# Per-buffer fills of the ones behind the probabilities, and a new issue order, in a fused attention and MLP kernel

## The chip, the core and the metric

The kernel runs on one core of a Trainium2 chip. The metric is the device time of one execution in microseconds (us). A core has a matrix engine (PE) that writes its products to eight accumulator banks, a vector engine (DVE), a scalar engine (ACT), a general engine (POOL) and a queue engine (SP) that only issues DMAs. Each engine takes its instructions strictly in the order in which the program lists them for it; engines wait for each other, and for DMAs, through semaphores.

## The reference

```python
scores = scale * np.matmul(q, k.transpose(0, 1, 3, 2))       # 4 batches, 8 heads, 768 x 64
# heads 0, 2, 6 ("retrieval"): causal mask
# other heads ("stream"): causal, and key < 4 or within 64 behind the query
a = softmax(where(mask, scores, -1e9))
x = matmul(a, v)                      # laid out as 3072 tokens x 512
h = x @ w_in                          # 512 -> 2048
g = np.maximum(h, 0.0) + alpha * np.minimum(h, 0.0)
out = g @ w_out                       # 2048 -> 512, float32
```

## The kernel before

The whole program is a list of small named steps, `ORDER`, written out by hand in the source. Each name is looked up in a table `I` and called, and the call emits the instructions of that step. As every engine is in order, `ORDER` fixes for each engine, and for the DMA queues of SP, ACT and POOL, what stands behind what. PSUM banks are handed out by age while the list is walked (`take`, `give`).

Heads are worked in pairs, four pairs for a batch: pair number n runs from 0 to 15, n modulo 4 chooses the heads (2,6), (1,5), (0,4) or (3,7), and n divided by 4 is the batch. The letters of a name tell the step:

- `Lq`, `Lk`, `Lv`: load q, k or v of a pair by DMA, nearly all from the SP queue, one or two DMAs for a head (L202 to L249). There are four buffers for each of the three. A stream head's v has a small extra DMA for its last 24 rows (L249), which waits for a fill of the buffer (`vz`).
- `Cq`, `Ck`, `Cv`: cast to bf16, on POOL for the first pairs, later mostly on DVE. A cast of v of a stream pair also copies the four sink rows (L312).
- `Tq`, `Tk`, then `tq`, `tk`: for n below 8, transpose on PE and copy out of the bank (DVE for the first pairs, ACT later). From n = 8 on, `Dq` and `Dk` do it by transposing DMAs on the SP queue (L328, L344).
- `S n.hh.m`, `s`, `m`: scores of a part on PE, exponential on ACT (L473, L521, L527), mask by a multiply on DVE. In batch 0 the scores use two pairs of banks in turn and the mask is added on PE. From n = 4 on, consecutive `S` steps are gathered into a burst; where both heads of the array's halves have enough columns, the burst interleaves them so that two 64-row products run side by side (L434), and otherwise it emits them one at a time (L427).
- `A`, `a`: probabilities times v on PE (L560), then reciprocal and multiply on DVE (L570, L571). The v tile has a column of ones, so the sum of each row comes with it.
- `X`, `x`: transpose the pair's result into `xT`, on PE with a copy on DVE (L585, L590), or by a transposing DMA on SP (L579) for n = 4 and 8 to 14.
- `P t.f`, `p`, `g`: for token block t (512 or 256 tokens, two blocks for a batch) and block f of 128 columns of w_in, four products on PE (L605), one for each head pair in the order (2,6), (1,5), (0,4), (3,7); then a relu on ACT (L610) and the combination on DVE (L617). For f below 6 of block 0 the four products are three steps: `.0` the first two pairs, `.1` the third, `.2` the fourth.
- `O t.s.u`, `o`: a quarter (four products) of the second matrix product (L625), and the copy and store of 128 tokens. `L0` to `L2` are the last 128 tokens in three column pieces (L644).
- `wi0` to `wi7`, `wo0` to `wo3`: the weights, by DMAs on the POOL queue that also convert to bf16 (L713, L717). `wi` number i holds columns 512*(i//2) and up, for one half of the 128 rows: `P t.4` to `P t.7` need `wi2` and `wi3`, `P t.0` to `P t.3` need `wi0` and `wi1`, and so on.
- `warm`, `busy`: products on a zero tile at the start. `kz`, `qz`, `vz`, `sz`, `vo`, `ro`, `so`, `nz`, `kfz`: fills of parts of buffers that no later step writes. `ms`, `mr`, `ns`, `nr`: masks.

`eR` (two buffers) and `eS` (three buffers) hold the probabilities of retrieval and stream heads. A product of a tile of 128 rows reads a few columns behind the last written one; those are filled with ones by `ro` and `so` at the start.

```python
    for name in ORDER:
        if not beside_burst(name):
            emit_burst()
        I[name]()
```

Of the kernel before, what the change touches and what calls it, by code (L numbers as in the profile page):

```python
# [11 lines left out]


ORDER = """
busy warm0 sz2 kz1 kz3 Lq0.0 zero Lq0.1 id kz0 Lk0 La kz2 Lk1 nms Cq0.0 nmr qz Tq0.0 Lq1 Ck0.0 qz0 warm1 Tk0.0 Lq2 Lk2
mr warm2 vz3 Ck0.1 Cq0.1 Ck1.1 tk0.0 m14.0.2 tq0.0 Lv0 Ck1.0 S0.0.1 Tk0.1 vz1 sz1 tk0.1 s0.0.1 Lk3 S0.0.0 Cq1 Tq0.1
Lv1 Cq2 vz0 Ck2.1 S0.0.2 Ck2.0 vz2 s0.0.0 tq0.1 Cv0 Ck3.0 Tk1 Lq3 Tq1 sz0 s0.0.2 Lq5 so tq1 S0.1.2 vo s0.1.2 S0.1.0
s0.1.0 Lv2 Tq2 S0.1.1 Ck3.1 tk1.0 tk1.1 S1.0.1 Tk2 s0.1.1 tk2.1 tk2.0 s1.0.1 S1.0.0 A0.0 Cv1 tq2 A0.1 a0.0 wi0 a0.1
s1.0.0 S2.1.1 S2.1.0 s2.1.1 Tk3 S2.0.0 Cq3 s2.1.0 m4.0.2 m10.0.2 X0 wi1 s2.0.0 Cv2 S2.0.1 S1.1.1 Cq5 x0 s2.0.1 Tq3
tk3.0 ro Lk4 s1.1.1 Ck4.1 S1.1.0 tk3.1 tq3 wi2 s1.1.0 A1.0 S2.0.2 A2.1 S3.1.1 a1.0 Lv3 Ck4.0 Cv3.0 a2.1 Lk5 A1.1  # L20
s2.0.2 idf s3.1.1 S3.1.0 A2.0 s3.1.0 S3.0.0 a1.1 X1 a2.0 S3.0.1 x1 s3.0.1 kfz1 s3.0.0 Tk4 Cv3.1 wi3 wi6 X2 m6.0.2 Tq5
x2 A3.1 P0.2.0 Lq6 tk4.0 a3.1 A3.0 P0.3.0 Ck5.0 Lq4 tk4.1 a3.0 wi7 P0.0.0 wi5 ms P0.1.0 Al kfz2 X3 Ck5.1 P0.1.1 Tk5
tq5 wi4 tk5.0 x3 P0.0.1 P0.2.1 P0.3.1 P0.1.2 P0.0.2 P0.3.2 Cq4 P1.2 al p0.1 g0.1 p0.3 Lk6 P0.2.2 P1.0 p0.2 g0.3 p1.0
g0.2 p0.0 g1.0 P1.6 P1.4 Lq8 p1.2 one Lq7 g1.2 nz1 wo1 nz0 Tq4 P0.6 wo0 P0.5.0 tk5.1 g0.0 P0.5.1 Lk7 P0.4.0 P0.4.1
p0.6 P0.4.2 g0.6 P0.5.2 p1.6 P0.14 g1.6 Cq6 Tq6 Ck6.0 p1.4 p0.14 g1.4 tq6 P0.13 p0.4 P0.10 g0.14 g0.4 p0.5 kfz0 P1.8
wo2 P0.9 Lv5 p0.13 tq4 g0.5 p1.8 g0.13 g1.8 p0.9 P0.11 Lv4 g0.9 p0.10 S4.0.4 S5.1.2 S4.1.3 Lv6 S4.0.0 p0.11 P1.10
s4.0.0 P0.8 P0.7 g0.10 g0.11 p1.10 S5.0.0 Lk9 g1.10 s5.1.2 p0.8 s4.0.4 g0.8 S4.1.1 S5.0.2 p0.7 S4.1.2 P0.12 s4.1.2 wo3
O0.1.0 s5.0.2 g0.7 s4.1.3 O0.1.1 Ck6.1 p0.12 S5.1.0 g0.12 m4.0.0 s4.1.1 S5.1.1 S4.0.3 m5.1.2 S5.0.1 Lq9 s5.0.0 S4.0.5
S4.1.4 Cv5 Cq7 s4.1.4 Lk8 m4.1.4 m5.0.0 Cq8 s5.0.1 P0.15 O0.3.0 s5.1.1 p0.15 s5.1.0 Tk6 Ck7.0 P1.14 g0.15 S4.1.5
s4.0.3 S4.0.1 s4.0.5 S4.1.0 S4.0.2 O0.3.1 O0.1.2 m5.1.1 m5.1.0 m4.0.4 s4.0.2 p1.14 m5.0.1 s4.1.0 Ck7.1 tk6.1 m4.1.3  # L30
m4.1.0 m5.0.2 O0.3.2 O0.0.0 tk6.0 Tk7 m4.1.1 A5.0 s4.0.1 A5.1 O0.0.1 g1.14 O0.0.2 Cv4 a5.0 Cv6 a5.1 Tq7 O0.3.3 tk7.0
O0.0.3 m4.0.3 O0.1.3 tk7.1 m4.0.5 m4.0.1 s4.1.5 o0.3 tq7 m4.1.5 o0.1 A4.1 S6.0.5 S7.0.0 o0.0 S6.1.2 S6.1.0 S7.0.2
S6.1.1 a4.1 A4.0 s6.1.1 S6.0.4 O0.2.0 s6.1.2 O0.2.1 s6.0.5 Lv7 m6.1.1 s7.0.0 s6.1.0 Cq9 Dq8 Ck8 m6.1.0 S6.0.0 s7.0.2
S7.1.0 s6.0.4 S7.1.2 S6.0.1 S7.1.1 S6.0.3 Dk8.0 m6.0.4 O0.2.2 s6.0.3 s7.1.0 m6.0.3 s7.1.2 X5 Dk8.1 P1.12 s6.0.1 m7.0.2
m6.1.2 Dq9 x5 m6.0.1 s7.1.1 m7.0.0 p1.12 Lv8 Ck9 a4.0 O1.1.0 m6.0.5 g1.12 Cv7 A6.1 ns s6.0.0 O0.2.3 S7.0.1 S6.0.2
m6.0.0 O1.1.1 S8.0.2 nr O1.1.2 s6.0.2 s7.0.1 Dk9.0 o0.2 A6.0 Lk10 S8.1.0 S8.0.1 m7.0.1 S8.0.3 s8.0.2 S8.1.1 S8.0.0
m7.1.0 a6.1 m7.1.1 S8.1.4 X4 s8.0.1 s8.1.4 a6.0 Dk9.1 Lq10 O1.1.3 s8.1.0 Lv9 A7.0 X6 m7.1.2 a7.0 kfz3 x6 s8.0.0 s8.1.1
A7.1 O1.0.0 O1.0.1 S9.0.0 S8.1.5 s8.0.3 S8.1.2 S9.0.2 o1.1 S8.0.4 a7.1 S8.1.3 X7 s8.1.3 Ck10 m8.1.0 s8.0.4 s8.1.5
O1.0.2 Lk11 s9.0.0 m8.0.3 O1.0.3 x7 P2.4 o1.0 m9.0.0 s8.1.2 S9.1.1 S9.0.1 m8.1.1 m8.1.5 p2.4 S9.1.2 S8.0.5 S9.1.0
m8.0.0 near0 m8.0.1 Lk13 s9.0.2 s8.0.5 s9.1.2 m8.0.4 P2.14 P2.2 s9.1.1 Cv8 s9.0.1 g2.4 m8.1.3 m8.1.4 A8.1 P3.10 P2.3  # L40
p2.2 P2.0 g2.2 Cq10 m8.0.5 a8.1 p2.14 g2.14 p2.0 m9.1.2 P2.1 g2.0 p2.3 P2.7 p2.7 p2.1 A8.0 P3.0 g2.3 P2.5 Ck11 g2.1
P2.9 p2.5 P2.6 g2.7 near2 g2.5 s9.1.0 p3.10 p3.0 p2.9 Cv9 g3.10 P2.8 Lq11 Dk11.1 g2.9 P3.8 m9.1.0 P2.10 p2.8 m9.1.1
Lk12 P3.4 g3.0 A9.1 near1 p2.6 g2.8 Lq13 P2.13 Cq11 P2.15 p2.13 Dk10.1 Dk10.0 Dq10 g2.6 p2.10 g2.13 p3.4 Lq12 P3.6
g2.10 P3.14 p2.15 a9.1 g2.15 P2.11 O2.0.0 P2.12 g3.4 O2.0.1 p2.11 p3.8 g2.11 Ck12 S10.0.1 S10.0.4 s10.0.1 g3.8 p3.14
O2.0.2 s10.0.4 Dk11.0 O2.1.0 Dq11 p2.12 a8.0 g3.14 S10.1.1 S10.0.0 p3.6 g2.12 m10.0.4 S10.1.0 S10.0.5 s10.1.0 s10.1.1
O2.1.1 Lv11 Cq12 O2.0.3 g3.6 S10.0.3 S11.0.0 m10.1.0 s10.0.5 s10.0.0 S11.1.2 S11.1.0 m9.0.2 S10.1.2 S10.0.2 s10.0.3
Cq13 O2.1.2 m10.0.0 s10.1.2 Lv10 Ck13 m9.0.1 m10.1.2 s11.1.2 m11.1.2 s11.1.0 Dk12.0 P3.2 s10.0.2 p3.2 A9.0 s11.0.0
# [24 lines left out]


@with_exitstack
def kernel(
    ctx: ExitStack,
    tc: tile.TileContext,
    q: bass.AP,
    k: bass.AP,
    v: bass.AP,  # L80
    is_retrieval: bass.AP,
# [652 lines left out]
    fill("qz", qT_all[:, :, S:S + 32].bitcast(fp32), 0.0)  # L734
    fill("qz0", qT_all[D:128, 0, 0:S].bitcast(fp32), 0.0)
    fill("vo", vb_all[:, :, :, :, D:D + 1], 1.0)
    fill("ro", eR_all[:, :, FAR.RTOT:E_R].bitcast(fp32), ONES)
    for i in range(NS):
        fill(f"sz{i}", eSv[:, i, :, 192:SLOT].bitcast(fp32), 0.0)
    fill("so", eS_all[:, :, 5 * SLOT + 192:6 * SLOT + 128].bitcast(fp32), ONES)  # L740
    item("idf", nc.vector.tensor_copy, ident_f, ident[0:16, 0:16])
    item("nms", sink_mask)
    item("nmr", causal_mask)
# [125 lines left out]
```

## Time and profile before

| | |
|---|---|
| median of 3 runs | 230.88 us (230.71 to 231.18) |
| span of the profiled execution | 230.0 us |
| what lies outside the span (median less span) | 0.9 us |
| PE | 221.2 us busy, 96% of the span, 1974 recorded products |
| DVE, ACT, POOL | 153.3 us (67%), 139.1 us (60%), 47.1 us (20%) |
| DMA | 36.62 MB, 159 GB/s over the span |
| granted PE clock | 1.000 |

A profile's span runs from the first to the last instruction of one execution, and the chain of waits is followed back from the last one. Products are pipelined and their ends are modelled, so a busy PE may still be waiting a little inside a step. A few per cent of the product records are missing; a hole of about 0.22 us between two products of 512 columns is such a missing record.

### The profile page before, as it was taken

What the parts mean: (1) busy time and instruction counts of PE and PEld (TensorE: products, weight loads), DVE (VectorE), ACT (ScalarE), POOL (GpSimd) and SP (SyncE); (2) the same over time, 40 slices, a digit from 0 to 9 for tenths busy, and PEclk for the clock granted to TensorE, in tenths of its full rate; (3) what the DMA queues carried; (4) which work ended last, traced back from release to release, by engine and by line L of the source; (5) the groups of instructions that cost most, each with busy time, mean ns of one, the idle gap of its engine ahead of it and who ended that gap; (6) DMA issues with size and microseconds to landing.
All of it is one profiled execution on the core that took longest, in us unless ns stands there. A gap on an engine that the chain in (4) does not pass through costs nothing.

```text
span 230.0 us, 5212 instructions
## 1 busy us (share of the span) xinstructions
PE 221.2 (96%) x1974; PEld 136.7 (59%) x2002; DVE 153.3 (67%) x396; ACT 139.1 (60%) x280; POOL 47.1 (20%) x96
## 2 busy tenths in 40 slices
PE   7989889999999999999999999999999999999994
PEld 7777857555566655565466445556854555554553
DVE  5688768997647866999997349979990345545110
ACT  6679647999968567554864874498422333623232
POOL 6658758000430643000002100010000020000000
PEclk9999999999999999999999999999999999999999
DMA  6979999999999999899979999893310130110033
GB/s 197 299 184 279 246 250 218 231 212 180 209 234 158 230 220 238 157 216 183 184 139 186 211 249 183 163 197 61 62 36 0 48 137 1 46 48 1 0 137 137
DMA packets 92448, 36.62 MB, mean 159 GB/s; under 512 B 79472, under 2 KB 90632, under 8 KB 92424
## 3 DMA queue, kind: packets, MB, share of 16 engines
q1 hardware_dynamic: 86168, 26.97, 59.7%
q0 software_dynamic: 5792, 8.93, 17.3%
q10 hardware_dynamic: 464, 0.40, 0.5%
q8 instruction: 15, 0.25, 0.5%
q14 instruction: 9, 0.07, 0.1%
HBM read 27.55 MB, written 6.29 MB: 147 GB/s over the span
## 4 chain that ended last, share of the span: by engine, by line
PE 85%; DMA 10%; SPq 1%; issue 1%; DVE 1%; POOL 0%; ACT 0%; DVEq 0%
PE P L605 36%; PE P L625 34%; PE P L560 6%; DMA vf<-in_v_dram 5%; DMA kf<-in_k_dram 4%; PE P L434 4%; PE P L644 2%; PE P L427 1%; PE P L585 1%; PE P L369 1%; SPq L247 1%; DVE vb L312 0%; SPq L224 0%; SPq L210 0%; DVE vb L349 0%
## 5 line engine op out<-in xcount | busy, mean ns | idle before, releaser
L617 DVE SCALAR_TENSOR_TENSOR g<-neg,oma,P 128x512 bf16<-128x512 f32 (+1 forms) x128 | 72.9, 610 | 39.7 <-ACT neg L610 38.6
L605 PE MATMUL P<-xT,w_in_b 128*128 128x256 bf16 (+1 forms) x503 | 89.5, 325 | 0.4
L610 ACT ACTIVATE neg<-P 128x512 f32<-128x512 f32 x96 | 54.3, 608 | 52.2 <-PE P L605 43.4
L625 PE MATMUL P<-w_out_b,g 128*128 128x512 bf16 x349 | 84.3, 379 | 1.5 <-issue 0.6
L605 PEld LDWEIGHTS <-w_in_b 128*128 128x128 bf16 x512 | 48.7, 98 | 32.4 <-DVE g L617 0.4
L625 PEld LDWEIGHTS <-g 128*128 128x128 bf16 x368 | 34.5, 98 | 36.8 <-issue 1.3
L473 ACT ACTIVATE eR<-P 128x448 bf16<-128x448 f32 (+6 forms) x63 | 36.6, 621 | 13.6 <-PE P L434 5.1
L635 POOL DMA_DIRECT2D out_dram<-ot x18 | 9.9, 553 | 117.5 <-ACT ot L631 117.5
L571 DVE TENSOR_TENSOR xn<-P,rcp 128x448 bf16<-128x448 f32 (+1 forms) x32 | 19.5, 608 | 1.1
L631 ACT COPY ot<-P 128x512 f32<-128x512 f32 x23 | 13.2, 594 | 11.0 <-PE P L625 8.6
L527 ACT ACTIVATE eS<-P 128x384 bf16<-128x384 f32 (+1 forms) x25 | 13.5, 570 | 3.4 <-PE P L505 2.6
L521 ACT ACTIVATE eS<-P 128x352 bf16<-128x352 f32 x30 | 13.8, 490 | 1.5 <-PE P L427 1.0
L560 PE MATMUL P<-vb,eS 128*128 128x65 bf16 x260 | 11.3, 193 | 1.5 <-DVE vb L312 0.8
L417 PE MATMUL P<-qT,kT 128*128 128x192 bf16 (+13 forms) x68 | 11.5, 251 | 1.1 <-ACT eR L473 0.6
L560 PEld LDWEIGHTS <-eS 128*128 128x128 bf16 x260 | 10.2, 97 | 3.5 <-issue 1.9
L570 DVE RECIPROCAL rcp<-P 128x7 f32<-128x7 f32 (+1 forms) x32 | 6.3, 197 | 7.2 <-PE P L560 6.9
L536 DVE TENSOR_TENSOR eS<-eS,ms_near 128x352 bf16<-128x352 bf16 x30 | 9.4, 336 | 2.3 <-ACT eS L521 2.2
L434 PE MATMUL P<-qT,kT 64*128 64x176 bf16 (+17 forms) x172 | 10.9, 250 | 0.0
L560 PEld LDWEIGHTS <-eR 128*128 128x128 bf16 x276 | 9.6, 97 | 1.5
L434 PEld LDWEIGHTS <-kT 64*128 64x128 bf16 x172 | 6.8, 94 | 6.0 <-issue 5.7
L560 PE MATMUL P<-vb,eR 128*128 128x65 bf16 x276 | 10.1, 193 | 0.0
L483 DVE TENSOR_TENSOR eR<-eR,mr_near 128x128 bf16<-128x128 bf16 (+5 forms) x36 | 6.9, 225 | 4.3 <-ACT eR L473 4.3
(104 smaller groups left out, 183.7 us busy)
## 6 DMA issues: line engine op xcount, KB each, us to landing
out_dram<-ot POOLq DMA_DIRECT2D x18, 256.0 KB, 3.7
vf<-in_v_dram SPq DMA_DIRECT2D x22, 192.0 KB
kf<-in_k_dram SPq DMA_DIRECT2D x21, 192.0 KB
qf<-in_q_dram SPq DMA_DIRECT2D x18, 192.0 KB
qf<-in_q_dram SPq DMA_DIRECT2D x7, 384.0 KB
w_in_b<-in_moe_w_in_dram POOLq DMA_DIRECT2D x8, 256.0 KB, 9.5
w_out_b<-in_moe_w_out_dram POOLq DMA_DIRECT2D x4, 512.0 KB, 13.6
kf<-in_k_dram SPq DMA_DIRECT2D x9, 196.0 KB
```

Of the source, the lines that this page charges most:

```text
L417: nc.tensor.matmul(to, keys, queries, start=True, stop=stop)
L434: nc.tensor.matmul(to, keys[own], queries[own], start=True, stop=True)
L473: nc.scalar.activation(ebuf[n, hh][:, lo:hi].rearrange("p (x c) -> p x c", x=len(parts)), P[:, got[0]:got[0] + len(parts), 0:(hi - lo) // ...
L521: nc.scalar.activation(slots, sc[:, 0:352].rearrange("p (s c) -> p s c", c=176), AF.Exp, scale=scale)
L527: nc.scalar.activation(slots, sc.rearrange("p x (s c) -> p x s c", c=192), AF.Exp, scale=scale)
L560: nc.tensor.matmul(pav[:, i, :], e[:, o:o + 128], vv[:, j, hh, 0:D + 1], start=(m == 0), stop=(m == len(terms) - 1))
L571: nc.vector.tensor_tensor(xn[n][:, 0:nt, D * hh:D * hh + D], pav[:, :, 0:D], rcp.to_broadcast([128, nt, D]), op=ALU.mult)
L605: nc.tensor.matmul(psg[:, w * i:w * (i + 1)], w_in_b[:, c, 128 * fb:128 * (fb + 1)], xT[:, c, o:o + w], start=(x == 0), stop=(x == 3))
L610: nc.scalar.activation(neg[t, f], bank(held["P", t, f][0]), AF.Relu, scale=-1.0)
L617: nc.vector.scalar_tensor_tensor(g_buf[t % 2][:, fb, 0:w], neg[t, f][:, c], oma[:, fb:fb + 1], bank(got[0])[:, c], op0=ALU.mult, op1=ALU.add)
L625: nc.tensor.matmul(bank(held["O", t, s][0]), g_buf[t % 2][:, f, 128 * s:128 * (s + 1)], w_out_b[:, f, :], start=(f == 0), stop=(f == 15))
L631: nc.scalar.copy(ot, bank(got[0]))
```

## The change

It does two things. The ones behind the probabilities are filled buffer by buffer: `ro` becomes `ro0` and `ro1`, `so` becomes `so0` to `so2`, each over the same columns of one buffer instead of all. And `ORDER` is replaced as a whole: the same steps, in another sequence. The numbers of products, exponentials, copies and DMAs are the same. No step's own code changes.

The sequence is long; shown are its beginning, up to the point where the token blocks of batch 0 begin, the two places further on of which the prediction speaks, and the end.

```diff
-    fill("ro", eR_all[:, :, FAR.RTOT:E_R].bitcast(fp32), ONES)
+    for i in range(NR):
+        fill(f"ro{i}", eR[i][:, FAR.RTOT:E_R].bitcast(fp32), ONES)
     for i in range(NS):
         fill(f"sz{i}", eSv[:, i, :, 192:SLOT].bitcast(fp32), 0.0)
-    fill("so", eS_all[:, :, 5 * SLOT + 192:6 * SLOT + 128].bitcast(fp32), ONES)
+    for i in range(NS):
+        fill(f"so{i}", eS[i][:, 5 * SLOT + 192:6 * SLOT + 128].bitcast(fp32), ONES)
...
-busy warm0 sz2 kz1 kz3 Lq0.0 zero Lq0.1 id kz0 Lk0 La kz2 Lk1 nms Cq0.0 nmr qz Tq0.0 Lq1 Ck0.0 qz0 warm1 Tk0.0 Lq2 Lk2
-mr warm2 vz3 Ck0.1 Cq0.1 Ck1.1 tk0.0 m14.0.2 tq0.0 Lv0 Ck1.0 S0.0.1 Tk0.1 vz1 sz1 tk0.1 s0.0.1 Lk3 S0.0.0 Cq1 Tq0.1
-Lv1 Cq2 vz0 Ck2.1 S0.0.2 Ck2.0 vz2 s0.0.0 tq0.1 Cv0 Ck3.0 Tk1 Lq3 Tq1 sz0 s0.0.2 Lq5 so tq1 S0.1.2 vo s0.1.2 S0.1.0
-s0.1.0 Lv2 Tq2 S0.1.1 Ck3.1 tk1.0 tk1.1 S1.0.1 Tk2 s0.1.1 tk2.1 tk2.0 s1.0.1 S1.0.0 A0.0 Cv1 tq2 A0.1 a0.0 wi0 a0.1
-s1.0.0 S2.1.1 S2.1.0 s2.1.1 Tk3 S2.0.0 Cq3 s2.1.0 m4.0.2 m10.0.2 X0 wi1 s2.0.0 Cv2 S2.0.1 S1.1.1 Cq5 x0 s2.0.1 Tq3
-tk3.0 ro Lk4 s1.1.1 Ck4.1 S1.1.0 tk3.1 tq3 wi2 s1.1.0 A1.0 S2.0.2 A2.1 S3.1.1 a1.0 Lv3 Ck4.0 Cv3.0 a2.1 Lk5 A1.1
-s2.0.2 idf s3.1.1 S3.1.0 A2.0 s3.1.0 S3.0.0 a1.1 X1 a2.0 S3.0.1 x1 s3.0.1 kfz1 s3.0.0 Tk4 Cv3.1 wi3 wi6 X2 m6.0.2 Tq5
-x2 A3.1 P0.2.0 Lq6 tk4.0 a3.1 A3.0 P0.3.0 Ck5.0 Lq4 tk4.1 a3.0 wi7 P0.0.0 wi5 ms P0.1.0 Al kfz2 X3 Ck5.1 P0.1.1 Tk5
...
+Lk0 ro0 zero nms m8.0.2 Lq0.0 Lk1 Ck0.0 id vo Ck0.1 kz1 busy nmr qz warm0 vz1 Ck1.0 sz0 ms m14.0.2 qz0 sz1 Cq0.0 kz3
+Ck1.1 La kz0 Tk0.0 tk0.0 kz2 Lq1 idf Cq1 mr Lq0.1 Tq0.0 tq0.0 warm2 so0 Tk0.1 warm1 S0.0.1 Tk1 tk0.1 tk1.0 Tq1 s0.0.1
+S0.0.0 Cq0.1 tq1 S0.0.2 Tq0.1 s0.0.0 Lk2 Ck2.1 sz2 Ck2.0 m4.0.2 Lq2 Cq2 Lv1 Cv1 Lk3 Ck3.0 tk1.1 wi0 Lv0 Ck3.1 tq0.1
+vz3 vz0 Cv0 Tk2 S1.1.0 s0.0.2 Tq2 S1.0.1 Lq3 s1.1.0 Cq3 Lk4 Ck4.0 s1.0.1 S1.1.1 s1.1.1 Ck4.1 S0.1.1 s0.1.1 S0.1.2
+s0.1.2 Lv3 so1 A1.1 so2 tk2.1 tk2.0 S0.1.0 Al s0.1.0 tq2 Tk3 kfz2 one a1.1 al tk3.0 S1.0.0 A0.0 Cv3.0 a0.0 wi3 S2.0.1
+s1.0.0 s2.0.1 tk3.1 Tq3 tq3 S2.1.0 s2.1.0 A1.0 S2.0.2 a1.0 vz2 Lv2 wi2 Cv2 wi1 s2.0.2 A0.1 a0.1 S3.1.0 s3.1.0 Cv3.1 X1
+x1 S2.0.0 s2.0.0 Lq4 Cq4 kfz0 X0 S3.1.1 nz1 x0 Tk4 s3.1.1 S2.1.1 A2.0 tk4.0 s2.1.1 A2.1 Lk5 Lk6 a2.0 S3.0.0 A3.1 a2.1
+ro1 S3.0.1 a3.1 wi4 Tq4 Lq7 s3.0.0 s3.0.1 A3.0 tq4 Ck5.0 wi5 Lq5 a3.0 X2 x2 S4.0.5 S4.0.4 Lk7 P0.4.0 tk4.1 X3 P0.4.1
+x3 P0.6 s4.0.4 p0.6 s4.0.5 P1.4 p1.4 P0.4.2 p0.4 P0.2.0 P0.2.1 P0.1.0 g0.4 g0.6 g1.4 ns wi7 P1.0 p1.0 Lq6 g1.0 P0.7
+Lv4 p0.7 wi6 P0.1.1 P0.0.0 P0.0.1 P0.1.2 p0.1 P0.2.2 p0.2 wo0 Ck5.1 Tk5 tk5.0 Ck6.0 g0.7 g0.1 g0.2 Ck6.1 P0.9 p0.9
+P0.3.0 P1.2 P0.11 p1.2 kfz1 P0.10 P0.0.2 Cq5 wo1 Lv5 p0.10 g0.9 g1.2 tk5.1 p0.11 g0.11 P0.3.1 P0.3.2 g0.10 P0.5.0
+P0.5.1 P1.14 nz0 p0.3 P1.8 p1.8 g0.3 g1.8 P1.10 P0.5.2 p0.5 p0.0 g0.0 Tq5 Cq7 p1.14 wo2 Lk9 Lk8 m8.1.2 g0.5 Lv7 Lq8
...
+s7.1.2 m7.1.2 m6.0.4 s6.1.0 O1.1.2 m6.1.0 m6.0.1 Cv7 A6.1 a6.1 m7.0.2 A6.0 A7.1 O0.0.2 a6.0 A7.0 X6 O1.1.3 Dk8.1 Dk9.0
+Lq9 X4 Dq8 a7.1 a7.0 x5 X7 O0.0.3 x7 x6 P2.1 p2.1 P2.15 p2.15 g2.1 P2.0 Dk8.0 Lk11 Lv11 P3.4 p2.0 g2.0 Cq9 Lk10 Lq10
...
+O3.1.0 O3.1.1 m10.0.0 Dq12 X9 O3.0.1 A11.1 A8.1 Lk13 m11.0.0 O2.3.2 A11.0 A10.0 a8.1 X8 O2.1.3 O3.0.2 O2.3.3 a11.0
+Cq15 a11.1 X11 a10.0 Ck12 Cq14 Ck13 O3.1.2 O3.1.3 O3.0.3 X10 Dq14 o2.3 P4.6 P4.0 p4.0 P5.12 g4.0 p5.12 g5.12 P4.5 p4.6
...
+o6.1 o6.2 O7.0.3 o6.0 o7.0 L0 l1 l0 L2 l2
```

## The prediction

> **What bounds the kernel now.** I read the page first, then the chain of waits in order of time, then what PE waited for, then the DMA queues by stretch and POOL's timeline.
>
> ```profile
> span 230.0 us, 5212 instructions
> PE 221.2 (96%) x1974; PEld 136.7 (59%) x2002; DVE 153.3 (67%) x396; ACT 139.1 (60%) x280; POOL 47.1 (20%) x96
> PE   7989889999999999999999999999999999999994
> DMA  6979999999999999899979999893310130110033
> ```
>
> PE has holes only in the first five or six slices and in the last. The chain says what they wait for (start, length, what):
>
> ```profile
> 7.65 6.60 DMA kf<-in_k_dram
> ...
> 15.13 5.14 DMA vf<-in_v_dram
> 20.28 7.32 DMA vf<-in_v_dram
> ...
> 27.69 0.60 DVE vb L349
> 28.31 1.05 DVE vb L312
> 29.40 0.50 PE P L560 x11
> ...
> 32.17 0.50 PE P L585 x7
> ```
>
> Up to 27.6 the chain is loads; v of pair 3 comes last, its cast and sink copy follow, and at 32.2 PE transposes that pair (X3). From there to 227.2 the chain is PE alone, and PE's longest waits there are 0.2 us, the size of a missing record. So the time is: the moment from which PE never stops, plus PE's remaining work, plus 2.8 us of tail (last product 227.2, span 230.0). An order can win only in the first 32 us, and can lose anywhere.
>
> The change moves loads and weights in that stretch, so I look at how the two DMA queues share the engines. First 33.5 to 38.0, where SP is nearly silent, then 48 to 54, where both are busy, then the weights' own row:
>
> ```profile
> q0 software_dynamic: 906, 0.87, 117.1%
> q1 hardware_dynamic: 111, 0.06, 6.2%
> q0 software_dynamic: 893, 0.89, 87.3%
> q1 hardware_dynamic: 925, 0.35, 33.5%
> DMA to landing us min/median/max: 7.1/9.5/11.0
> ```
>
> Alone, POOL's queue (q0) moves 906 packets in 4.5 us, 201 per us; beside SP's (q1) 893 in 6 us, 149, packet for packet. From 21.5 to 26 it was 513 in 4.5 us (114), from 27.5 to 34 it was 616 in 6.5 us (95). A `wi` is 0.25 MB of the 0.87 MB that 906 packets carry: 256 packets, so 1.3 us alone and 2.2 to 2.7 us beside loads. From its issue to its landing it takes 7.1 to 11.0 us.
>
> **The fills.** One fill of 128x328 at 332 ns becomes two of 128x164; rows of 128x128 (165 ns) and 128x192 (218 ns) give about 0.2 us each. One of 128x288 at 298 ns becomes three of 128x96, between the 85 ns of a 128x32 and the 165 ns: about 0.14 each. Together +0.2 us on DVE. What counts is where they stand: `ro0`, `vo` and a `kz` (0.2, 0.12, 0.8 us) now precede `busy`, so the warm-up products start at about 2.2 instead of 1.06; they and the transposes behind them end near 8.5. ACT's fill `kz2` (1.68) now precedes `tq0.0`, which ends near 8.1 instead of 6.45. The first exponential starts at 9.05 instead of 8.35. ACT then has 20.3 us of work from 5.1 to the last exponential of batch 0, summed from its rows (0.88 for 896 columns, 0.81 for 768, 0.5 for 384, 0.8 for a copy of q): it could end at 25.4. With A3.0 (0.5), the divide (0.85) and X3 (0.4), that allows X3 to end at 27.2, so ACT is not last.
>
> **The loads.** SP's order up to q2 holds the same pairs, so v1, now seventh, lands when v0 did: POOL takes it at 12.8. Before, k3, v1, q3, q5, v2, k4, v3 and two weights (3.2 MB) landed from there to 27.6, with SP blocked on the way. Now k3, v0, q3, k4, v3, v2 and `wi0` are wanted: 2.56 MB, 10.1 us at the 251 to 260 GB/s of the stretches 18:24 and 24:30. So v3's first head lands near 20.5 and v2 near 22.9. Lq5 has moved behind; the tail of v2 waits for `vz2`, behind a1.0 on DVE, near 21, and q4, k5 and so on are queued behind it on SP. They are first needed at Tq4, near 27.
>
> **POOL, which issues the weights.** From 12.8, in its new order: Cv1 0.93, sinks 0.63, Ck3.0 0.5, `wi0` 0.77, Ck3.1 0.5, Cv0 0.93, Cq3 0.83, Ck4 1.0, a fill 0.2: 19.1. Then it waits for v3 until 20.5; cast and sinks 0.9: 21.4. `wi3` is issued at 21.4, `wi2` at 22.0, and Cv2 with its sinks ends at 24.2. From there: A2.0 0.65, A2.1 0.4, S3.0.0 0.65, two exponentials 1.3, A3.0 0.5, divide 0.85, X3 0.4, that is X3 ending at 28.9.
>
> But P0.4.0 stands ahead of X3 on PE, and it is the first step with weights, `wi2` and `wi3`. Issued at 22.0, `wi2` lands between 29.1 (the shortest 7.1 us) and 31.5 (the median). I take 30.8, nearer the median, since q4, k5, k6 and q7 are all in SP's queue then. P0.4.0 (0.43) and X3 (0.4) follow: X3 ends at 31.6.
>
> The Trainium skill (DMA: Bandwidth & Descriptors, Anatomy of one DMA — SWDGE (gpsimd) path) puts such a DMA at 2.0 us plus its bytes at 436 GB/s, which for 0.25 MB would be an estimate of 2.6 us. By it the weights would be there at 24.6, X3 would end at 28.9 and the sum would be near 228.9. The row above, 7.1 us at least, decides against it.
>
> **What X3 at 31.6 is worth.** Before, X3 ended at 32.5, and PE had done eight token products ahead of it (P0.2.0, P0.3.0, P0.0.0, P0.1.0: 8 x 0.217 = 1.73). Now it has done two (0.43) and two unpaired score groups of 448 columns (0.42 ns a column, 0.39). So 0.9 us more is left behind X3, and the new X3 must end at 31.6 to draw level. It does, to within a microsecond either way: 0.0, bounds -1.7 (`wi2` at 29.1) to +0.7 (at 31.5).
>
> **Bursts.** The issue lists hold 35330 columns in paired score products (L434) and 6662 in single ones (L427); now 33441 and 8551. 1889 columns lose their partner: 1889 x 0.42 ns / 2 = +0.4 us on PE, which is the path. Bounds 0.2 (pairs are seldom even) to 0.4.
>
> **Batch 1 to batch 2.** Behind A7.0, PE has X6, a quarter, X7 and a quarter (2.5 us); DVE in that time has a7.0, x5, x7, x6 (0.85 + 3 x 0.55 = 2.5) and starts late by its semaphore: P2.1 waits 0.2. Bounds 0 to 0.7, for masks queued ahead on DVE.
>
> **Batch 2 to 4.** All four X of batch 2 are DMAs, as before. Behind A10.0, PE has six quarters and the first half of P4.6: 5.6 us. DVE does a11.0, Cq15, a11.1, a10.0 and ends 2.5 us behind A10.0; X10 is the last of the SP queue, 1.25 us to issue. How long a transposing DMA takes to land no row says; the last before, issued at 169.56, was used by a product at 174.34 without a wait, so at most 4.8 us. X10 lands 3.8 to 7.3 us behind A10.0: a wait of 0 to 1.7; I take 0.3. In batch 3 X12 is issued 1.5 us behind A12.1 with 5.1 us of PE work: at most 6.3, so nothing to 1.2; I take nothing.
>
> **Elsewhere.** In the middle, 24 P units now run nearly alone: 0.87 us of PE for 0.61 us of ACT and 0.61 (0.87 for the short blocks) of DVE; DVE also takes six casts of some 0.55 there, 24 x 0.7 + 3.3 = 20 for PE's 20.8, with eight banks of slack. The S stages carry 33 exponentials of 0.5 to 0.6 (18 us) for some 20 us of PE. Nothing. The last product is still a 128-column piece with its copy and store behind it: tail 2.8, give or take 0.3 (l0's store is nearer).
>
> **Sum.** 0.0 + 0.4 + 0.2 + 0.3 = +0.9 on the span, 230.9; the median lies 0.9 above the span, so 230.88 + 0.9 = **231.8**. The likeliest case's own range is 230.9 to 233.2.
>
> **Rivals.**
> - *The weights come early (faster).* If `wi2` lands at 29.1, X3 ends at 29.9, 1.7 earlier; with bursts at 0.4 and hidden transitions: 230.88 - 1.7 + 0.4 = 229.6. It decides from `wi2` landing before 30.3. For it: less is wanted before v2, and POOL issues `wi3` and `wi2` 2 to 6 us earlier than the third and fourth weight before. Against: SP's queue is no longer blocked, so it shares every packet.
> - *The weights fall behind (slower).* SP has nine pairs unblocked behind v2, which before were held. At 114 packets per us `wi1`, `wi5` and `wi6` land at 33.0, 37.5 and 42.0, due at X3 plus 2.2, 6.6 and 11.8, so 33.8, 38.2 and 43.4. At 95 they are late by up to 0.9; at 70, a quarter below the lowest row, `wi5` is 3.6 late: 231.8 + 3.6 = 235.4. It decides below 100 packets per us.
> - *It does nothing:* loads, weights and ACT meet where they did, and the transitions are hidden. 230.9.
>
> **Chances.** Forecast 0.42, early weights 0.32, late weights 0.15, nothing 0.11. A measurement of this kernel can tell about 0.2%, 0.46 us, from no change. Below 230.4: the early weights and a little of the others, 0.33. Within: nothing, and the forecast's lower edge, 0.17. Above: 0.50. The range for 8 in 10 runs from 229.2 (early weights with the tail's 0.3) to 235.0.
>
> **What would show it.** The chain after should end its loads near 23, and the last thing released before PE's unbroken run should be a product of L605 that waits for w_in. X3 (L585) near 31. L434 with 158 products, L427 with 46. Waits of PE for an xT transpose near 85 and 135 of at most a microsecond. I am wrong if PE waits more than 1 us anywhere after 45, if the unbroken run starts with v or an exponential as its releaser, or if it starts before 29.5 or after 33.

## The result, and the profile after

The changed kernel takes **245.32 us** (median of 4 runs, 244.15 to 247.53) against 230.80 of the kernel before: the ratio is 1.0658, 95% interval 1.0586 to 1.073. The forecast was 231.8 with a range of 229.2 to 235.0. The sign was right; the size was wrong by a factor of sixteen.

The page of the changed kernel, in the parts that were shown of before (its profiled execution took 246.04, its span is 244.3):

```profile
span 244.3 us, 5199 instructions
PE 226.9 (93%) x1974; PEld 139.3 (57%) x2002; DVE 155.6 (64%) x399; ACT 141.1 (58%) x280; POOL 47.7 (20%) x96
PE   5999879999989997799989987999999999999995
PEclk9999979999999999799999997999999999999999
DMA  6997999999924999999947799993521141010023
```

Before, PE's row had nothing below 9 from the seventh slice to the last but one. Now it has holes in slices 12, 16 and 17, 21, 24 and 25 (a slice is 6.1 us), and the row of the granted clock, whose mean was 1.000 before, has three dents, in slices 6, 17 and 25. What PE waited for, longest first (line, releaser, total us, times, longest):

```profile
PE P L605 <- DVE g L617: 3.0, 1, 3.0
PE P L605 <- DMA w_in_b<-in_moe_w_in_dram: 2.6, 1, 2.6
PE P L605 <- DMA xT<-xn: 2.5, 1, 2.5
PE P L708 <- DVE busy L294: 2.5, 1, 2.5
PE P L560 <- DVE eS L534: 0.5, 1, 0.5
```

The fourth is the warm-up products at the start, which wait for their fill; before it was 1.1 us, and the prediction expected 2.2. By the count of columns that follows it leaves after 1.1 us behind at 10 us and 0.1 at 21, so it is no part of the loss.

The chain of waits was before PE alone from 32 us on. Now it can be followed back only to 117 us, and up to 148 it runs in good part through VectorE, ScalarE, SP and two transposing DMAs. Two pieces of it (start, length, what):

```profile
134.94 1.21 SPq L328
136.19 4.76 DMA xT<-xn
144.24 3.72 DMA xT<-xn
```

For that count, and to see where the 14.3 us between the two spans arise, I added up the columns of the recorded products and compared the times at which both kernels had issued the same amount. After is behind by 2.5 us at 37 us of its own time, by 3.1 at 68, 4.3 at 75, 4.9 at 94, 9.7 at 105, 9.1 at 117, 10.6 at 125, 15.3 at 154, and 14.3 at the end. So there are five places: the head (2.5), and waits near 71, 96, 122 and 145.

**The head.** `wi3` and `wi2` are issued at 22.6, and the first product that reads them starts at 32.15 (in brackets: what the engine waited for):

```profile
22.62 1.24 POOL L713 DMA_DIRECT2D w_in_b<-in_moe_w_in_dram  x2
...
32.15 0.63 PE L605 MATMUL P<-xT,w_in_b 128*128 128x512 bf16 x1 [2.61 <-DMA w_in_b<-in_moe_w_in_dram]
```

**Near 96 and near 122.** These waits begin on VectorE, whose queue is in order. First SP's issue of q10, then the casts of q10 and of q13, each with VectorE's idle time ahead of it:

```profile
91.68 1.09 SPq L213 DMA_DIRECT2D qf<-in_q_dram  x2
...
97.31 0.56 DVE L321 CAST natq<-qf 128x768 bf16<-128x768 f32 x1 [3.79 <-DMA qf<-in_q_dram]
...
120.51 0.56 DVE L321 CAST natq<-qf 128x768 bf16<-128x768 f32 x1 [2.35 <-issue]
```

The load of q10 stands behind three others on SP and lands 5.6 us after its issue began; VectorE reaches its cast 1.8 us after that issue and stands still for 3.8 us. Queued behind the cast are gated blocks (L617). Each of them holds a PSUM bank (the memory that products are written to), so the next product (L605) waits for "DVE g". For q13's cast the profile names no releaser. In the code its buffer is the one that the transpose of q11 reads, and SP issued that transpose at 117.6 behind three others, so I take this for the cause. In the order before, q10's load stood 70 steps ahead of its cast, k10's 43; now it is 11 and 13.

**Near 71.** One mask of 128x384 took 2.46 us where the others take 0.35 (durations of the 15 in ns, min/median/max), in the time in which POOL cast two tiles:

```profile
L534 DVE TENSOR_TENSOR eS<-eS,ms x15: 345/351/2459, 61.7 to 84.0; 128x384 bf16<-128x384 bf16 x15
```

```profile
68.48 3.29 DVE L534 TENSOR_TENSOR eS<-eS,ms 128x384 bf16<-128x384 bf16 x3 [3.32 <-ACT eS L527]
68.90 1.82 POOL L354 CAST vb<-vf 128x896 bf16<-128x896 f32 x2
```

**Behind the long waits** the products are slow. Busy times by stretch (us, then PE, PEld, DVE, ACT, POOL, the granted clock, DMA share, GB/s):

```profile
28.16:31.57 3.41, 1.38 (x22) 0.93 (x18) 1.58 (x4) 2.12 (x4) 2.01 (x5) 1.00 1.19 234
31.57:34.98 3.41, 2.83 (x12) 1.62 (x14) 0.56 (x1) 0.00 (x0) 3.09 (x12) 0.50 1.17 253
...
96.43:99.84 3.41, 0.72 (x7) 0.65 (x7) 2.53 (x6) 0.00 (x0) 0.00 (x0) 1.00 1.38 220
99.84:103.25 3.41, 3.41 (x14) 1.84 (x13) 2.04 (x5) 1.73 (x4) 0.00 (x0) 0.50 1.15 202
...
144.21:147.62 3.41, 1.30 (x7) 0.48 (x5) 1.01 (x3) 0.00 (x0) 0.12 (x1) 1.00 1.00 216
147.62:151.04 3.42, 3.04 (x9) 1.26 (x9) 0.00 (x0) 0.28 (x1) 0.00 (x0) 0.50 1.03 206
```

Three times the clock is halved for 3.41 us, directly behind 3.41 us in which PE was busy for 1.4 us or less. If half of the busy time in them is lost, that is (2.83 + 3.41 + 3.04) / 2 = 4.6 us of the 14.3, an estimate. The mean granted clock says the same: (1 - 0.979) x 244.3 = 5.1 = three windows of 3.41 at half speed.

### The profile page after: what moved, and what is told of

It reads as the page before. It is cut to its first block, busy times and chain, and to the rows that moved or that the text cites. A ratio compares the mean times of both kernels' runs of the same rounds, so it can differ in the third digit from the quotient of the medians.

```text
span 244.3 us, 5199 instructions
## 1 busy us (share of the span) xinstructions
PE 226.9 (93%) x1974; PEld 139.3 (57%) x2002; DVE 155.6 (64%) x399; ACT 141.1 (58%) x280; POOL 47.7 (20%) x96
## 4 chain that ended last, share of the span: by engine, by line
PE 41%; DMA 3%; DVE 3%; issue 2%; ACT 1%; SPq 1%; DVEq 0%
PE P L605 17%; PE P L625 17%; DMA xT<-xn 3%; PE P L560 3%; PE P L434 2%; PE P L644 1%; DVE vb L354 1%; DVE eR L483 1%; DVE natq L321 1%; PE P L427 1%; SPq L328 1%; DVE xn L571 0%; ACT eR L473 0%; ACT eS L521 0%; DVE eS L536 0%
## 5 line engine op out<-in xcount | busy, mean ns | idle before, releaser
L605 PE MATMUL P<-xT,w_in_b 128*128 128x256 bf16 (+1 forms) x503 | 89.9, 335 | 8.5 <-DVE g L617 3.0
L617 DVE SCALAR_TENSOR_TENSOR g<-neg,oma,P 128x512 bf16<-128x512 f32 (+1 forms) x128 | 71.0, 609 | 38.6 <-ACT neg L610 38.5
L605 PEld LDWEIGHTS <-w_in_b 128*128 128x128 bf16 x512 | 51.0, 100 | 43.7 <-issue 12.3
L625 PEld LDWEIGHTS <-g 128*128 128x128 bf16 x368 | 33.8, 98 | 35.3 <-issue 0.7
L635 POOL DMA_DIRECT2D out_dram<-ot x18 | 10.4, 579 | 146.9 <-ACT ot L631 146.8
L631 ACT COPY ot<-P 128x512 f32<-128x512 f32 x23 | 13.7, 603 | 14.9 <-PE P L625 14.9
L434 PE MATMUL P<-qT,kT 64*128 64x176 bf16 (+15 forms) x158 | 10.8, 253 | 0.8 <-ACT eS L521 0.4
L534 DVE TENSOR_TENSOR eS<-eS,ms 128x384 bf16<-128x384 bf16 x15 | 7.5, 519 | 3.3 <-ACT eS L527 3.3
```

Of the source, the lines that this page charges most:

```text
L434: nc.tensor.matmul(to, keys[own], queries[own], start=True, stop=True)
L605: nc.tensor.matmul(psg[:, w * i:w * (i + 1)], w_in_b[:, c, 128 * fb:128 * (fb + 1)], xT[:, c, o:o + w], start=(x == 0), stop=(x == 3))
L617: nc.vector.scalar_tensor_tensor(g_buf[t % 2][:, fb, 0:w], neg[t, f][:, c], oma[:, fb:fb + 1], bank(got[0])[:, c], op0=ALU.mult, op1=ALU.add)
L625: nc.tensor.matmul(bank(held["O", t, s][0]), g_buf[t % 2][:, f, 128 * s:128 * (s + 1)], w_out_b[:, f, :], start=(f == 0), stop=(f == 15))
L631: nc.scalar.copy(ot, bank(got[0]))
```

## The experiments

All kernels carry the new fills. Their edits are in `ORDER`; e7, e14 and e16 also add a step to the code. Their line numbers are one less than those of after (L604 for L605). The ratio is to the kernel before, run beside them. One more order, e3 (that of before up to `g1.2`, near 38 us, then the rest as in after), was meant to take the late head away alone. It has no time: in that order the engines wait for one another for ever (a deadlock).

| run | median us | before | ratio, 95% interval |
|---|---|---|---|
| e1, fills alone | 230.39 | 231.00 | 0.999 (0.996 to 1.002) |
| e2, head of after, rest of before | 243.67 | 231.00 | 1.053 (1.046 to 1.060) |
| e4, casts later | 244.16 | 231.00 | 1.056 (1.051 to 1.062) |
| e5, loads earlier | 240.22 | 230.46 | 1.039 (1.031 to 1.047) |
| e6, transposes earlier | 243.16 | 230.46 | 1.051 (1.042 to 1.061) |
| e7, PE kept busy | 245.16 | 230.46 | 1.060 (1.050 to 1.070) |
| e8, head, first try | 248.36 | 230.46 | 1.073 (1.063 to 1.083) |
| e9, middle mended | 235.63 | 230.05 | 1.022 (1.016 to 1.029) |
| e10, head and middle | 236.63 | 230.05 | 1.025 (1.018 to 1.032) |
| e11, head of before, middle mended | 239.65 | 230.83 | 1.034 (1.025 to 1.043) |
| e12, head of before, rest of after | 248.22 | 230.83 | 1.077 (1.069 to 1.084) |
| e13, longer head of before, middle mended | 235.25 | 231.53 | 1.017 (1.011 to 1.022) |
| e14, loads held | 236.35 | 231.45 | 1.023 (1.018 to 1.029) |
| e15, POOL's casts earlier | 243.38 | 231.45 | 1.051 (1.043 to 1.058) |
| e16, weights first | 239.19 | 230.67 | 1.038 (1.034 to 1.042) |

**e1: the fills alone.**

```diff
-... Lq5 so tq1 ... tk3.0 ro Lk4 ...
+... Lq5 so0 so1 so2 tq1 ... tk3.0 ro0 ro1 Lk4 ...
```

> The issue order of before, with the three small changes to the fills alone: ro0, ro1 stand where ro stood, so0, so1, so2 where so stood. Theory (the fills are nothing, the order is all): 0.2 us more of VectorE work beside loads, 230.9 give or take 0.5. Rival (a fill per buffer sits on a longer chain than it looks): up to 245.

Measured 0.999 (0.996 to 1.002). The fills cost nothing that can be measured, so the loss is the order's.

**e2: the head of after, then the order of before.** All steps of after up to `x3`, then what is left in the order of before.

> The order of after up to the copy of pair 3's transposed rows (x3, near 34 us), then everything that is left in the order of before (two exponentials of pair 4 are pulled ahead so that a bank is free). Theory (the losses are local to where TensorE waits): only the late weights with the slow products behind them remain, 2.5 us by the traces at equal TensorE work: 233.4, 232.5 to 234.5. Rival (the late head shifts the loads, and the waits of the middle come from that): above 238.

Measured 243.67, which by its number is the rival's; the waits say why it is neither. The two orders don't fit together: at the seam PE waits once, for POOL's cast of a q.

```profile
PE P L368 <- POOL natq L320: 6.9, 1, 6.9
PE P L559 <- POOL vb L353: 2.5, 1, 2.5
```

Behind the seam PE waits nowhere over 0.2 us. So a late head alone makes none of the later waits; the total measures the seam.

**e4: the two casts later.**

```diff
-... P2.4 p2.4 Cq10 Ck10 g2.4 P2.11 p3.14 g3.14 g2.15 ... g3.10 P2.3 p2.3 g2.3 Dk10.1 ...
+... P2.4 p2.4 g2.4 P2.11 p3.14 g3.14 g2.15 ... g3.10 P2.3 p2.3 g2.3 Cq10 Ck10 Dk10.1 ...
-... s8.0.2 Cq13 O2.0.3 ... A8.0 O2.1.0 Dq13 ...
+... s8.0.2 O2.0.3 ... A8.0 O2.1.0 Cq13 Dq13 ...
```

> The order of after, with VectorE's casts of q10 and k10 moved behind four more gated blocks (to just ahead of the transposing DMA that reads them) and the cast of q13 moved behind A8.0. Theory (VectorE's queue is held by a cast whose load has not landed, the blocks behind it keep their PSUM banks, and TensorE runs out of banks): the wait of 3.2 us near 96, the slow products behind it (1.1) and the 1.5 near 122 go: 245.3 - 5.8 = 239.5, 238.5 to 241. Rival (the loads themselves are late, so whoever needs them waits in the casts' place): 243 to 246.

Measured 244.16: the rival's range. The 1.5 us near 122 went, as expected. But the one near 96 came back 6 us later, in two parts:

```profile
PE P L604 <- DVE g L616: 2.1, 2, 1.3
```

Now VectorE is held by k10's cast, which takes 1.97 us there instead of 0.62 (the last section shows what ran beside it), and by q11's, which waits 1.1 us for its load. With loads as late as these, moving the casts only moves the place.

**e5: the loads earlier.**

```diff
-... Dk8.0 Lk11 Lv11 P3.4 p2.0 g2.0 Cq9 Lk10 Lq10 Lv10 Dq9 Dk9.1 Lq11 Lv9 ...
+... Dk8.0 Lv11 P3.4 p2.0 g2.0 Cq9 Lv10 Dq9 Dk9.1 Lv9 ...
-... wo3 Lv6 O0.2.0 ... Cv5 kfz3 S5.1.1 ...
+... wo3 Lv6 Lk10 Lq10 Lq11 O0.2.0 ... Cv5 kfz3 Lk11 S5.1.1 ...
```

> The order of after, with the loads of k10, q10, q11 moved up behind the load of v6 (near 50 us instead of 90) and that of k11 behind its fill kfz3 (near 71). The casts stay where they are. Theory (the four pairs of batch 2 are queued on SP only 5 us ahead of their casts on VectorE, which hold up the gated blocks behind them): the wait near 96 us (3.2) and the slow products behind it (1.1) go: 245.3 - 4.3 = 241.0, 240 to 242.5. Rival (v10, v11, k9 or the transposes take the place of those loads at the same moment): 243.5 to 246.

Measured 240.22, 5.1 us less than after, within the theory's range. The same casts in VectorE's timeline, at the same place of its queue, now without a wait ahead of them, and PE has none between 80 and 106:

```profile
92.30 0.55 DVE L320 CAST natq<-qf 128x768 bf16<-128x768 f32 x1
92.77 0.62 DVE L339 CAST natk<-kf 128x896 bf16<-128x896 f32 x1
```

**e6: the transposes earlier.**

```diff
-... A9.1 a9.1 m10.1.2 ... Dq12 X9 O3.0.1 ...
+... A9.1 a9.1 X9 m10.1.2 ... Dq12 O3.0.1 ...
-... O2.3.3 a11.0 Cq15 a11.1 X11 a10.0 Ck12 ... O3.0.3 X10 Dq14 ...
+... O2.3.3 a10.0 X10 a11.0 Cq15 a11.1 X11 Ck12 ... O3.0.3 Dq14 ...
```

> The order of after, with the transposing DMA of pair 9's result (X9) moved up to right behind its divide, ahead of the loads and the transpose of pair 12's q, and pair 10's last divide and its transpose moved ahead of pair 11's. Theory (a11.0 waits for the buffer that X9 reads, X9 stands behind the cast and the transpose of q12, and X10 is last): the wait near 145 us falls from 2.7 to about 1 us, too short for slow products: 245.3 - 1.7 - 1.2 = 242.4, 241.5 to 243.5. Rival (a transposing DMA takes 4 to 5 us wherever it stands, and X11 is now the last): no less than 244.8.

Measured 243.16, within the theory's range. The wait near 145 fell from 2.5 to

```profile
PE P L604 <- DMA xT<-xn: 0.5, 1, 0.5
```

and no slow products follow it. The chain that made it in after is thereby named: VectorE's `a11.0` waited 1.7 us for the buffer that X9 was reading, X9 stood on SP behind the cast and the transpose of q12, and X10 came last of all.

**e7: PE kept busy in its wait.** The code gets a step of 44 products that nothing reads.

```diff
+    def keep_warm(n):
+        got = take(*ANY)
+        for i in range(n):
+            nc.tensor.matmul(bank(got[0])[:, 0:128], busy, busy, start=True, stop=True)
+        give(got)
+    item("keep", keep_warm, 44)
-... X10 Dq14 o2.3 P4.6 ...
+... X10 Dq14 o2.3 keep P4.6 ...
```

> The order of after, with 44 products of 128 columns on a tile of zeros put in front of the first block of token block 4 (P4.6), where TensorE waits 2.7 us near 145 us; nothing reads what they give. Theory (a wait of over 2.5 us costs its length and then about 1.1 us more, because the granted clock falls to a half for the next 2.5 us of products): the wait stays, the products behind it take 0.22 instead of 0.43 us and the granted clock there is 1: 245.3 - 1.1 = 244.2. Rival (the products are slow because what they read arrives slowly): 245.3, six products of 0.43 us behind the wait.

The total, 245.16, can't tell 1.1 us (its runs spread over 4 us). The stretches can:

```profile
146.03:149.44 3.41, 3.41 (x50) 2.85 (x49) 0.45 (x1) 0.00 (x0) 0.00 (x0) 1.00 1.01 216
149.44:152.86 3.42, 3.42 (x21) 1.96 (x20) 1.39 (x3) 1.87 (x4) 0.00 (x0) 1.00 1.33 160
```

Behind the wait, which is filled, the granted clock is 1.00, and 21 products fit where after had 9. The products of 128x512 among them took 379 ns on average, in after 626. Near 34 and 102, where nothing was filled, the same execution shows 0.50 and 0.75. The slow products are the clock, not the data.

**e8: the head, first try.**

```diff
-... vz3 vz0 Cv0 ... Lq3 s1.1.0 Cq3 Lk4 Ck4.0 s1.0.1 ... Ck4.1 ...
+... vz3 vz0 vz2 Cv0 ... Lq3 s1.1.0 Cq3 s1.0.1 ...
-... Tk3 kfz2 one ... a0.0 wi3 S2.0.1 ... a1.0 vz2 Lv2 wi2 Cv2 wi1 ...
+... Tk3 wi3 wi2 kfz2 one ... a0.0 S2.0.1 ... a1.0 Lv2 Lk4 Cv2 Ck4.0 Ck4.1 wi1 ...
```

> The order of after, with its first 30 us eased: the fill of v2's tail (vz2) before the loads, k4's load and casts behind v2's, and the weights wi3 and wi2 issued while POOL waits for v3. Theory (TensorE waits at 28 us for what comes last of v2, wi2 and wi3, and all three stand behind k4 and behind a fill): TensorE is dense 2 us earlier and its clock does not fall there: 245.3 - 2 - 1 = 242.3, 241.5 to 243.8. Rival (the queues are full in any order, so what is moved ahead delays v3 and v2 by as much): 244.5 to 246.5.

Measured 248.36, worse than either. I had forgotten who else waits: the transposes of k4 stand ahead of all of batch 0's last products on PE, and k4 now came last.

```profile
PE P L368 <- POOL natm L333: 4.1, 1, 4.1
```

**e9: the middle mended.** e5 and e6 together, `Cq13` as in e4, and

```diff
-... wo3 Lv6 O0.2.0 ... m5.1.2 Cv4 O0.1.0 ... m4.0.1 Cv5 kfz3 ...
+... wo3 Lv6 Lk10 Lq10 Lq11 Cv4 Cv5 O0.2.0 ... m5.1.2 O0.1.0 ... m4.0.1 kfz3 Lk11 ...
```

> The order of after with the edits of the two runs before put together (loads of pairs 10 and 11 earlier, X9 and pair 10's end earlier), the cast of q13 behind A8.0, and POOL's casts of v4 and v5 moved ahead of the first product with the second weights, so that they no longer run beside VectorE's masks near 69 us. The first 34 us are those of after. Theory (the four middle waits are separate and each is local): 245.3 - 5.1 (near 96) - 3 (145, with its slow products) - 1.3 (122) - 0.9 (70; the mask that took 2.46 us takes 0.35 again) = 235.0, 234 to 236.5. Rival (the waits are one shortage of loads or of VectorE, which comes back elsewhere when pushed away): above 238.

Measured 235.63: 9.7 of the 14.5 us are back. From 60 us to the end PE waits once, for 0.6 us, for xT. The profiled execution grants full clock throughout. What is left lies ahead of 60 us. PE's waits from 15 to 60 us in e9:

```profile
PE P L368 <- POOL natq L320: 1.7, 1, 1.7
PE P L604 <- DMA w_in_b<-in_moe_w_in_dram: 1.5, 2, 0.8
PE P L559 <- POOL vb L353: 1.1, 1, 1.1
```

In e1, which has the order of before, PE waits in this stretch once, for 0.2 us. 4.3 less 0.2, and 0.6 for xT, and 0.4 for products without a partner (below), is 5.1 of the 5.6 by which e9 is above the kernel before.

**e15: POOL's casts earlier, alone.** Only the move of `Cv4` and `Cv5`.

> The order of after, with POOL's casts of v4 and v5 alone moved ahead of the first product with the second weights. Theory (VectorE's mask of 384 columns took 2.46 us near 69 because POOL cast two tiles beside it): the longest of the 15 masks takes no more than 0.5 us, TensorE's waits near 71 (0.6 and 0.3) go: 245.3 - 0.9 = 244.4. Rival (the mask waited for something else, an exponential or a bank): one mask again over 2 us.

```profile
L533 DVE TENSOR_TENSOR eS<-eS,ms x15: 344/351/498, 62.7 to 84.1; 128x384 bf16<-128x384 bf16 x15
```

The longest mask takes 0.50, and PE waits for no mask there. The total, 243.38, is 1.9 lower than after; 0.9 was expected, and the runs of one kernel differ by more than the rest, so the total can't tell the size.

**e10: head and middle.** e9 and another head: `vz2`, `Lk4` and k4's casts as in e8, `wi3`, `wi2` and `wi1` issued while POOL waits, and `Tk4`, `Tq4` and their copies behind `x3`.

> The run before, and a new first 34 us: vz2 before the loads, k4's load and casts behind v2's, wi3, wi2 and wi1 issued while POOL waits for v3 and v2, and pair 4's transposes of q and k moved behind X3 on TensorE, since k4 and q4 now come later. Theory (what is left of the loss, 2.5 us, is the first 34 us, where the loads and weights that X3 needs stood behind others that it does not): 235.0 - 2.5 = 232.5, 231 to 233.5. Rival (the order of the transfers cannot help, since all of them are needed within 10 us): 234.5 to 237.

Measured 236.63: the rival. The weights came in time; v2's cast did not:

```profile
PE P L559 <- POOL vb L353: 2.5, 1, 2.5
```

**e14: loads held.** e9, with SP held by a fill of two elements. It was to last until near 29 us; SP's next load was issued at 31.31.

```diff
+    item("hold", nc.vector.memset, kf[2][:, 0, 0, 0:2], 0.0)
-... A2.1 Lk5 Lk6 a2.0 ... Tq4 Lq7 s3.0.0 ... X2 x2 S4.0.5 S4.0.4 Lk7 P0.4.0 ...
+... A2.1 Lk5 a2.0 ... Tq4 s3.0.0 ... X2 x2 hold Lk6 Lq7 Lk7 S4.0.5 S4.0.4 P0.4.0 ...
```

> The mended middle (e9), with the loads of k6, q7 and k7 held on SP until pair 2's transposed rows are copied (near 29 us): a fill of two elements of k6's buffer on VectorE stands there, and the loads are queued behind it. Theory (the weights wi3 and wi2 land late because SP's loads take every second packet): TensorE's waits for weights at 28 to 36 us (1.5 in e9) go, X3 comes 1 to 2 us earlier: 235.6 - 1.5 = 234.1, 233 to 235. Rival (v2 and the weights end together, so the wait passes to v2's cast; or the held loads are missed later): 235.2 to 237.

Measured 236.35: the rival. No product waits for weights at 28 to 36 us any more, and one waits near 44 for the last of them:

```profile
PE P L604 <- DMA w_in_b<-in_moe_w_in_dram: 1.9, 1, 1.9
PE P L368 <- POOL natq L320: 1.0, 1, 1.0
PE P L559 <- POOL vb L353: 0.9, 1, 0.9
```

**e16: weights first.** As e14, but `hold` and the loads of k6, q7, k7 and q6 behind `g1.4`, k6's casts behind `wo2`, and `wi7` and `wi6` ahead of `ns`.

> The mended middle (e9), with the loads of k6, q7, k7 and q6 held until the gated block g1.4 (near 37 us), k6's casts moved behind wo2, and the weights wi7 and wi6 issued ahead of POOL's near masks (ns) instead of behind them. Theory (three pairs and the masks stand ahead of weights that are wanted first): the waits for weights at 28 to 45 us go (1.5 in e9, 1.9 in e14), and nothing takes their place: 235.6 - 2.5 = 233.1, 232 to 234.3. Rival (from 20 to 55 us all transfers are wanted, so a load that is held is missed later): 235.2 to 237.5.

Measured 239.19, above both ranges, and on the rival's side. No product waits for weights, but v2's cast is late here too, and gated blocks are:

```profile
PE P L559 <- POOL vb L353: 3.0, 1, 3.0
PE P L624 <- DVE g L616: 1.9, 1, 1.9
```

**e11, e12 and e13: the head of before.** All steps of before up to `g0.0` (e11, e12) or `g0.5` (e13), then the rest in the order of e9 (e11, e13) or of after (e12).

> The order of before up to the divide-free first gated block of column 0 (g0.0, near 42 us), then everything that is left in the order of the mended middle. Theory (what is left of the loss in that run sits in the first 42 us): before, and 0.4 for the products that lost their partner, and 0.7 for the wait that is left near 139: 230.4 + 1.1 = 231.5, 230.7 to 232.8. Rival (what is left is spread over the order in places too small to see): 234 to 236.

> The same head, then everything that is left in the order of after as it is. Theory (head and middle are independent): the head's loss goes, 4.1 by the runs so far (235.6 - 230.4 - 1.1), and the waits near 70, 96, 122 and 145 stay: 245.3 - 4.1 = 241.2, 239.5 to 243. Rival (the middle waits come from the late head): 231 to 236.

> The order of before up to the gated block g0.5 (near 47 us, with pair 6's q and k already cast), then everything that is left in the order of the mended middle: the seam of the two runs before, where TensorE waited 3 us near 50 for the cast of q6, is gone. Theory (what the mended middle still loses against before sits in its first 42 us): before and 0.4 for the products that lost their partner and 0.7 for the wait near 139: 231.7, 230.8 to 233. Rival (it is spread over the order): 234 to 236.5.

By their totals e11 (239.65) and e12 (248.22) lie above both of their ranges, and e13 (235.25) in its rival's. None of this decides, for the reason of e2: at the seam near 50 us PE waits for the cast of q6 (2.9 us in e11 and e12, 2.4 in e13), and half clock follows. They don't isolate the head. e12 does settle one thing. With the head of before, the waits of the middle stand as they were:

```profile
PE P L604 <- DVE g L616: 3.5, 1, 3.5
PE P L604 <- DMA xT<-xn: 2.3, 1, 2.3
PE P L559 <- DVE eS L533: 0.5, 1, 0.5
```

They come from the order of the middle itself.

## Why the prediction was wrong, step by step

**"Elsewhere. ... Nothing."** This is the step that failed most: it put the middle of the kernel at nothing. It weighed only busy times: PE, ACT and DVE per unit, and found slack. It did not look at where each load stands on SP against its cast on VectorE, nor at what POOL does beside VectorE. The cast of q10 stops a queue whose busy time is low; the blocks behind it hold the banks, and PE stops too. Measured: 3.0 near 96, some 1.5 near 122, 0.9 near 71, against nothing; with these waits and the one of the next step taken away, e9 has 9.7 us of the loss back. The order alone would have told the first (11 steps instead of 70).

**Batch 2 to 4: 0.3, bounds 0 to 1.7.** The mechanism was named, X10 as the last of SP's queue, and mis-sized: 2.5 us, outside the bounds. The sum had let VectorE do `a11.0` and `a11.1` without a wait; `a11.0` waited for X9's buffer. Three buffers of xn for four pairs are in the code, and I had not counted them.

**A step that was not there: the clock.** Each of the three long waits was followed by 3.41 us at half clock, 4.6 us together. The prediction's own sign of being wrong, a wait of PE of more than 1 us anywhere after 45, came true three times, but it had no price for what follows such a wait. The Trainium skill (TensorE: Matmul & The Clock Gate, What's actually happening) describes such a window of 3413 ns that runs free of the program and halves the rate behind an idle one; the prediction did not weigh it, since it forecast no such wait.

**`wi2` at 30.8, X3 ending at 31.6, worth 0.0.** v3 was there at 21.7 instead of 20.5, so POOL issued `wi3` and `wi2` 1.2 us later than in the sum; the product that reads them started at 32.15, and X3 ended near 33.3. The order of the steps (P0.4.0 as the last releaser, of which the prediction said that it would show the forecast right) was as told; X3 was foreseen near 31. The mis-sized term is the rate of the loads: 251 to 260 GB/s were taken from 18 to 30 us of before, and 211 were moved from 15 to 21.5 of after. With the clock the head cost 2.5 instead of 0.0. Runs of this same head show how close the next limit lies: in e15's profile it is v2's cast that PE waits for, 2.5 us, and the weights cost 0.3.

**What held.** POOL took v1 at 12.8 as told. Score products: 158 in pairs and 46 single, and PE's busy time is 223.3 us in e9 against 222.8 in e1, 2002 recorded products in each, which fits the 0.4 for the lost partners. The fills: nothing. That the sign of the whole came out is mostly luck: of the 0.9 forecast 0.4 is borne out, and the loss came from places that were put at nothing or nearly so. Batch 1 to batch 2: no wait near 85, inside 0 to 0.7. Tail: 3.1 us from the start of the last product to the end, in both kernels.

**The rivals.** "The weights come early" and "it does nothing" are out. "The weights fall behind" had the right sign and the wrong place: no weight behind the first two was waited for. None of the cases held a wait of VectorE for a load. One sum in "the weights fall behind" is short: at 70 packets per us `wi6` would be later still than `wi5`, by 5.7 us against 3.6. Nothing measured rests on it.

**What stays open.** e9, in which the middle is mended, is still 5.6 us above the kernel before, and some 4 us of that are waits ahead of 60 us. The traces show them as waits for v2, for weights and for pair 5's q. Four ways of reordering the transfers there (e8, e10, e14, e16) only moved the wait from one to the other. That would fit a stretch in which transfers are the limit: in after the DMA row is at 9 from the fifth slice to the eleventh, 24 to 67 us. But it is not shown. From 20 to 56 us after moves 213 GB/s and e14 215, while the kernel before moves 228 there without such waits. Which steps of the new head cost the 5 us was not isolated.

## What to carry to other kernels

When an order is changed, busy times are not enough. For every load, compare its place on the issuing queue with the place of the first instruction that reads it on an in-order engine, and ask what is queued behind that instruction and which buffers it holds. Count the buffers of every rotating tile against the number in flight around a stage's end. In this kernel a wait that left TensorE busy for 1.4 us or less of a window of 3.41 us cost up to 1.7 us beyond its length (an estimate, half of such a window); where a kernel's mean granted clock is below 1, look for those waits first.

## What the runs showed of the hardware

**The clock goes by windows.** In after the clock was halved three times, each time for 3.413 us. The starts, 31.57, 99.84 and 147.62, lie on one grid: they are 20 and 14 times 3.413 us apart. The skill's page speaks of an idle window; here a window with PE busy for 1.38 of 3.41 us was enough. And a longer wait can be cheaper: in e6, 2.9 us of waiting near 94 fell across two windows and left the clock alone, while two waits near 120, 1.8 and 0.3 us, fell in one window and the next was halved.

```profile
92.20:95.61 3.41, 2.09 (x14) 1.25 (x13) 0.21 (x1) 1.09 (x3) 0.54 (x1) 1.00 1.37 219
95.61:99.02 3.41, 1.82 (x13) 1.24 (x13) 3.10 (x7) 0.60 (x1) 0.00 (x0) 1.00 1.16 192
119.50:122.92 3.42, 1.25 (x14) 0.55 (x13) 2.65 (x14) 1.99 (x6) 0.00 (x0) 1.00 0.37 82
122.92:126.33 3.41, 3.41 (x38) 2.20 (x35) 0.97 (x4) 2.80 (x8) 0.00 (x0) 0.50 0.31 62
```

I laid this grid over the profiled executions that have halved windows, from 27 us on. All 18 windows at full clock with PE busy for 1.4 us or less were followed by a halved one; of three with 1.5 to 1.7 us (e11, e13, e14) two were, and of those with 1.71 us or more none. So the limit lies near 1.5 us here.

The same kernel can take 1 to 3 such windows: the four runs of after had mean clocks of 0.979 to 0.993. That does not explain their spread of 3.4 us, since the fastest run had 0.984 and the slowest 0.986.

**VectorE can stand still beside POOL.** A mask with two operands in SBUF took 2.46 us while POOL cast two tiles (0.95 us each), and 0.50 at most when the casts stood elsewhere (e15). It took 2.46 in all seven profiled executions in which these casts ran beside it. Over all 17 there are 255 such masks: the 177 with no instruction of POOL beside them took 0.36 us at most, and 45 of the other 78 took more than 0.40. Gated blocks, which read PSUM, did not: those of 512 columns took 0.75 us at most with POOL beside them (59) and without. e4 has a second case: of its eight casts of k in SBUF one took 1.97 us, the one beside a mask that POOL made in 1.28 us, and 0.62 + 1.28 is 1.9.

```profile
L339 DVE CAST natk<-kf x8: 607/618/1971, 62.5 to 165.8; 128x896 bf16<-128x896 f32 x8
```

```profile
100.24 1.28 POOL L679 TENSOR_SCALAR_AFFINE_SELECT mr_near<-one 128x1248 bf16<-128x1248 bf16 x1
```

The Trainium skill (SBUF — State Buffer, SBUF: two separate sides) tells of a pair of ports that the two engines lock for a whole instruction; both rows agree with that, and no run here shows the lock itself.
